# One PSUM bank for four products of a Winograd-style layer, and a unit's last additions spread over three quads

## The chip, the core and the metric

The kernel runs on one core of one Trainium2 chip. The core has a matrix engine (TensorE, "PE" in the profile, with its weight loads as "PEld"), VectorE ("DVE"), ScalarE ("ACT"), GpSimd ("POOL") and SyncE ("SP", here a queue for transfers). Each engine works through its own instructions in order, and engines wait for each other by semaphores. The metric is the device time of one execution in microseconds; lower is better.

## What is computed

Two layers in a row. The first filters each of 8 sequences along its length in the frequency domain; the second is a two-layer perceptron with an ELU between.

```python
# x: (8, 3008, 256), filt_r, filt_i: (1505, 256), w_in: (256, 2048), w_out: (2048, 256)
X = np.fft.rfft(x, axis=1)
y = np.fft.irfft(X * (filt_r + 1j * filt_i)[None], n=3008, axis=1)
h = y.reshape(8 * 3008, 256) @ w_in
g = np.where(h > 0, h, np.exp(np.minimum(h, 0)) - 1)
out = g @ w_out
```

Everything is float32; the two weight matrices and the filter arrive in the types that the kernel converts or gathers from.

## The kernel before

**The perceptron.** Both products are done by a 2 x 2 block scheme with seven products in place of eight (Strassen-Winograd). The rows of one batch are cut into six *units* (`m` = 0 to 5) of 2 x 256 rows (the first of 2 x 224), and the hidden width of 2048 into four parts (`q`). One combination of batch, unit and part is an *item*; there are 192. For an item, `up_steps` (line 296) gives seven steps s1 to s7 for the products P1 to P7 of the first layer, and `down_steps` (line 371) seven steps for the products of the second; below they are D1 to D7. One step is two matmuls of 128 x 128 weights with 256 columns, which the chip runs as four matmul records.

The seven first-layer products have to be added up. Before, P1 goes to PSUM tile pha and ScalarE copies it to t1; P2 is accumulated onto P1 in pha, which gives b11; P6 goes to phb and VectorE adds t1, giving t2; P5 goes to phc and VectorE adds t2, giving t4; P3 is accumulated in phc, and VectorE adds t2, giving b12; P7 goes to phd and VectorE adds t4, giving b22; P4 is accumulated in phd, and VectorE adds t2, giving b21. `add` is line 315. An accumulating step may write its tile only after whatever read the earlier sum there is done. On each of b11, b12, b22 and b21 the ELU runs as two ScalarE operations (`elu_exp`, lines 321 and 322: a Relu of -x, then an exponential) and one VectorE operation (`elu_max`, line 326). Four more VectorE operations (lines 359 to 363) combine these into the operands of the second layer's products: after them D1 takes b11, D2 b21, D3 b22, D4 t4, D5 t1, D6 t2 and D7 b12.

The second layer accumulates over the four parts `q` in four PSUM tiles po0 to po3. At the last part (`q == 3`), ScalarE copies po0 and po1 to k0 and k1 (line 387), VectorE makes one add (line 390) and, in the tail, six more (line 401) that give the unit's result c. `o_unit` (line 417) transposes c on VectorE (line 421) and issues 16 output transfers on SP.

**The order.** It is written out by hand. A loop over *quads* (line 626) runs the up steps of item i mixed with the down steps of item i - 1, by two strings of U and D; between the strings comes what a plan holds for "place 0" of that quad, and after the tails of both what it holds for "place 1". Since the down steps lag by one, unit m's last down steps run in the quad that is the next unit's first, numbered 4m + 4 within the batch's 24 quads.

```python
for k in "UDUDUDUUD": ...   # s1 D1 s6 D3 s2 D5 s5 s7 D7
                            # place 0
for k in "UDUDD": ...       # s3 D6 s4 D2 D4
                            # up_tail, down_tail, place 1
```

The plan spreads the filter layer of the following batch over the quads of this one: `a_unit` (first transform, place 0 of quads 0, 2, 3, 4, 6, 7), `b_unit` (second transform and the filter's four VectorE products, place 1 of quads 9 to 16), `bi_unit` (first half of the inverse, place 1 of quads 11 to 18), and `n_unit` (its second half and the rows' combination for one unit: 16 short matmuls, two ScalarE copies called y, four VectorE operations; place 0 of quads 8, 12, 16 and 20, place 1 of quads 1 and 5). `o_unit` stands at place 0 of quad 4m + 5 (counted from the batch's own start). The y rows that `n_unit` needs are read by `y_read` one or two quads ahead on the SP queue. In the first quads the conversion of the last weights (`w_convert`) and three memsets stand at place 1 of quads 0, 1 and 4.

**PSUM.** Eight banks: po0 to po3 hold one each, and a pool of four, `psM`, gives one to each of the other tiles in turn; every tile takes the buffer that was taken longest ago, and waits for its readers.

Of the kernel before, what the change touches and what calls it, by code (L numbers as in the profile page):

```python
# [95 lines left out]
def kernel(  # L96
# [30 lines left out]
    yd = pool("yd", 2, space=DRAM)  # L127
    fdp = pool("fdp", 1, space=DRAM)
    psO = pool("psO", 1, space=PSUM)
    psM = pool("psM", 4, space=PSUM)  # L130

    gb, gr, gi = (glob.tile([P, 2, 64], FP32, name=n) for n in ("gb", "gr", "gi"))

# [7 lines left out]

    def raw(src, row, ap, col=0):
        return bass.AP(tensor=src.tensor, offset=src.offset + row * D + col, ap=ap)

# [14 lines left out]
    def a_unit(b, c):  # L159
        t = t1s[b, c] = t1p.tile([P, XC, D], FP32, tag="t1", name="t1")  # L160
        xt, w = xs.pop((b, c)), tas.pop((b, c))
        for r in (0, 2):
            ps = psM.tile([P, 2, D], FP32, tag="mx", name="psa")
            for u in range(2):
                nc.tensor.matmul(ps[:, u, :], w[:, r + u, :], xt[:, r + u, :], start=True, stop=True)  # L165
            nc.scalar.activation(out=t[:, r:r + 2, :], in_=ps, func=AXT.Copy)

# [43 lines left out]
    def b_unit(b, g, f=None):  # L211
        t = t2s.pop((b, g))
        f = fbufs[(b * NG + g) % FBUFS] if f is None else f
        re, im = (psM.tile([P, 2, D], FP32, tag="mx", name=n) for n in ("psr", "psi"))
# [9 lines left out]
        nc.vector.tensor_tensor(out=q, in0=im, in1=f[:, 0], op=ALU.mult)  # L224
        nc.gpsimd.tensor_tensor(out=sr, in0=sr, in1=p, op=ALU.subtract)  # L225
        nc.gpsimd.tensor_tensor(out=si, in0=si, in1=q, op=ALU.add)
        ss[b, g] = (sr, si)

    def bi_unit(b, g):
        s = ss.pop((b, g))  # L230
        t = t3s[b, g] = t3p.tile([P, 4, D], FP32, tag="t3", name="t3")
        pa, pb = (psM.tile([P, 2, D], FP32, tag="mx", name=n) for n in ("pva", "pvb"))
# [4 lines left out]
        nc.scalar.activation(out=t[:, 2:4, :], in_=pb, func=AXT.Copy)  # L237

    def y_write(b, g):
        if g == 0:  # L240
# [16 lines left out]
    def n_unit(b, m):  # L257
        t, w, h = t4s.pop((b, m)), tns.pop((b, m)), half(m)
        rows = []
        for dh in range(2):  # L260
            y = yp.tile([P, 512], FP32, tag="y%d" % dh, name="y%d" % dh)
            ps = psM.tile([P, 512], FP32, tag="mx", name="psn")
# [3 lines left out]
            nc.scalar.activation(out=y[:, 0:2 * h], in_=ps[:, 0:2 * h], func=AXT.Copy)  # L266
            rows += [y[:, 0:h], y[:, h:2 * h]]
        s = yp.tile([P, 3, 256], FP32, tag="ys", name="ys")
        ys[b, m] = combine(*rows, *(s[:, i, 0:h] for i in range(3)))
# [23 lines left out]
    UPS = (1, 6, 2, 5, 7, 3, 4)  # L293
    DOWNS = (1, 3, 5, 7, 6, 2, 4)

    def up_steps(b, m, q):
# [7 lines left out]
        banks = {}  # L304

        def mm(n, key, start):
            if start:
                banks[key] = psM.tile([P, 2, 256], FP32, tag="mx", name="ph" + key)
            for a in range(2):
                nc.tensor.matmul(banks[key][:, a, 0:h], w_in[q][:, COMBO[n], a, :], y[n],  # L310
                                 start=start and a == 0, stop=True, skip_group_check=True)
            return banks[key][:, :, 0:h]

        def add(o, i0, i1):
            nc.vector.tensor_tensor(out=g[o], in0=i0, in1=i1, op=ALU.add)  # L315

        es = {}

# [8 lines left out]


        def s1():
            nc.scalar.activation(out=g["t1"], in_=mm(1, "a", True), func=AXT.Copy)  # L330

        def s6():
            add("t2", mm(6, "b", True), g["t1"])

        def s2():
            p = mm(2, "a", False)
            elu_exp("b11", p)
            elu_max("b11", p)

        def s5():  # L340
            add("t4", mm(5, "c", True), g["t2"])

        def s7():
            add("b22", mm(7, "d", True), g["t4"])
            elu_exp("b22", g["b22"])

        def s3():
            add("b12", mm(3, "c", False), g["t2"])
            elu_max("b22", g["b22"])

        def s4():
            elu_exp("b12", g["b12"])
            add("b21", mm(4, "d", False), g["t2"])

        def tail():
            elu_exp("b21", g["b21"])
            elu_max("b12", g["b12"])
            t1, b12, b22 = g["t1"], g["b12"], g["b22"]
            nc.vector.tensor_tensor(out=t1, in0=b12, in1=g["b11"], op=ALU.subtract)  # L359
            nc.vector.tensor_tensor(out=b12, in0=b22, in1=b12, op=ALU.subtract)  # L360
            elu_max("b21", g["b21"])
            nc.vector.tensor_tensor(out=g["t2"], in0=b22, in1=t1, op=ALU.subtract)
            nc.vector.tensor_tensor(out=g["t4"], in0=g["b21"], in1=g["t2"], op=ALU.subtract)
            g_of[b, m, q] = {1: g["b11"], 2: g["b21"], 3: b22, 4: g["t4"], 5: t1, 6: g["t2"], 7: b12}

        return (s1, s6, s2, s5, s7, s3, s4), tail


    PLACE = {1: (0, 0), 5: (0, 1), 3: (1, 0), 7: (1, 1), 2: (2, 0), 6: (2, 1), 4: (3, 0)}
# [1 line left out]
    def down_steps(b, m, q):  # L371
# [7 lines left out]
        def step(n):  # L379
            i, u = PLACE[n]  # L380
            for a in range(2):

                nc.tensor.matmul(po[i][:, u, 0:h], w_out[q][:, COMBO[n], a, :], g[n][:, a, :],  # L383
                                 start=q == 0 and a == 0 and n in (1, 3, 6, 4), stop=True, skip_group_check=True)
            if q == 3 and n in (5, 7):
                t = k[i] = kp.tile([P, 2, 256], FP32, tag="k%d" % i, name="k%d" % i)
                nc.scalar.activation(out=t[:, :, 0:h], in_=po[i][:, :, 0:h], func=AXT.Copy)
                if n == 7:
                    p3 = t[:, 0, 0:h]
                    nc.vector.tensor_tensor(out=p3, in0=p3, in1=k[0][:, 1, 0:h], op=ALU.add)  # L390

        def tail():
            if q != 3:
# [6 lines left out]
            def add(o, i0, i1):  # L400
                nc.vector.tensor_tensor(out=o, in0=i0, in1=i1, op=ALU.add)  # L401

            add(c12, po[2][:, 1, 0:h], p1)
            add(c11, po[2][:, 0, 0:h], p1)
            add(p7, p7, c12)
            add(c12, c12, p35)
            add(c21, po[3][:, 0, 0:h], p7)
            add(c22, p7, p5)
            cs_[b, m] = c

        return [(lambda n=n: step(n)) for n in DOWNS], tail

# [1 line left out]

    def o_unit(b, m):
        c = cs_.pop((b, m))
# [97 lines left out]
    with tc.manual_schedule():  # L516
# [81 lines left out]
        for b in range(B):  # L598
# [20 lines left out]
            for m, (s, place) in enumerate(((20, 0), (25, 1), (29, 1), (32, 0), (36, 0), (40, 0))):  # L619
                if b > 0 or m > 0:  # L620
                    at(t + s - (1 if m == 0 else 2), 0, y_read, b, m)
                    at(t + s, place, n_unit, b, m)
                at(t + PER + 4 * m + 5, 0, o_unit, b, m)

        items = [(b, m, q) for b in range(B) for m in range(6) for q in range(4)]
        for i in range(-PER, len(items) + 2):
            ups, up_tail = up_steps(*items[i]) if 0 <= i < len(items) else ((), None)
            downs, down_tail = down_steps(*items[i - 1]) if 1 <= i <= len(items) else ((), None)
            ups, downs = list(ups), list(downs)
            for k in "UDUDUDUUD":  # L630
                s = ups if k == "U" else downs
                if s:
                    s.pop(0)()
            for fn, a in plan.get((i, 0), ()):
                fn(*a)
            for k in "UDUDD":
                s = ups if k == "U" else downs
                if s:
                    s.pop(0)()
# [38 lines left out]
```

## Time and profile before

| what | value |
|---|---|
| median of 3 runs | 2736.13 us (2735.93 to 2737.07) |
| the profiled execution | 2735.2 us |
| its span, first to last instruction | 2733.4 us |
| first P1 of the first quad starts | 132.86 us |
| last matmul ends | 2721.3 us |
| mean granted clock of TensorE | 0.978 |

In the profile's group rows stand line, engine, operation, tiles (output, then inputs), shape and count; behind the first bar the busy time in us and the mean of one in ns; behind the second the engine's idle time just before them and what ended most of it. Matmul rows overlap, as a matmul starts before its predecessor has drained: the pace of TensorE is the distance from start to start, not the duration. In the timeline, "x4" says that four records were merged into one row. Half of the matmul records are of the second layer (L383), most of the rest of the first (L310).

```profile
L383 PE MATMUL po<-g,wo 128*128 128x256 f32 (+1 forms) x5376 | 1325.1, 375 | 0.0
L310 PE MATMUL pha<-y,wi 128*128 128x256 f32 (+1 forms) x1536 | 396.2, 380 | 9.3 <-ACT g L330 9.2
L322 ACT ACTIVATE e<-e 128x512 f32<-128x512 f32 (+1 forms) x768 | 477.5, 622 | 24.3
L326 DVE SCALAR_TENSOR_TENSOR g<-e,g 128x512 f32<-128x512 f32 (+1 forms) x576 | 387.0, 672 | 12.9 <-ACT e L322 12.8
```

### The profile page before, as it was taken

Reading aid. Unit: us, or ns where it says so; the run is one execution under the profiler, and the core shown is the slowest. Engines: PE = TensorE matmul, PEld = TensorE weight load, DVE = VectorE, ACT = ScalarE, POOL = GpSimd, SP = SyncE. Lnnn points to the kernel's source line nnn. Section 1 sums busy time; section 2 is a strip of 40 time slices with the busy share of each in tenths; the row PEclk is TensorE's granted clock in tenths of the full one; section 3 lists DMA queues with packets and bytes.
Section 4 is the critical chain, followed back from the end, with each engine's and each line's share of the span. In section 5 each row is a group of like instructions: output and inputs, shape, how many; then the busy total and the mean of one; then the engine's idle time right before and its main releaser. Section 6 shows DMA issues by size and latency. Waiting matters only on the chain.

```text
span 2733.4 us, 36388 instructions
## 1 busy us (share of the span) xinstructions
PE 2626.5 (96%) x12992; PEld 2237.5 (82%) x12992; DVE 2066.9 (76%) x3531; ACT 1286.0 (47%) x2177; POOL 275.6 (10%) x325
## 2 busy tenths in 40 slices
PE   2689999999999999999999999999999999999998
PEld 1278778987899878998789877898789987898887
DVE  3877877778777777768876787777877777777876
ACT  2244454544545444454444445454454544444443
POOL 4311210002000120001200021000210012000000
PEclk7599999999999999999999999999999999999999
DMA  9645321434114331242323333143421323110100
GB/s 244 180 116 122 88 69 37 110 96 102 43 42 121 78 93 37 74 120 68 79 50 88 88 85 73 37 110 97 98 57 41 79 62 95 37 39 19 26 22 16
DMA packets 229428, 214.47 MB, mean 78 GB/s; under 512 B 131620, under 2 KB 192566, under 8 KB 229248
## 3 DMA queue, kind: packets, MB, share of 16 engines
q1 hardware_dynamic: 210592, 173.65, 25.8%
q0 software_dynamic: 17792, 36.93, 5.6%
q8 instruction: 103, 1.69, 0.3%
q10 hardware_dynamic: 864, 1.57, 0.2%
q14 instruction: 77, 0.63, 0.1%
HBM read 136.97 MB, written 78.12 MB: 79 GB/s over the span
## 4 chain that ended last, share of the span: by engine, by line
PE 77%; DVE 12%; ACT 5%; DMA 2%; issue 2%; POOL 0%; DVEq 0%; SPq 0%; ACTq 0%; POOLq 0%
PE po L383 34%; PE pha L310 11%; PE phc L310 10%; PE phd L310 10%; PE phb L310 5%; DVE g L315 3%; PE psa L165 3%; ACT e L322 2%; ACT e L321 2%; PE pva L209 2%; PE psn L264 2%; PE psr L209 2%; DVE c L401 2%; DVE g L326 1%; DVE g L359 1%
## 5 line engine op out<-in xcount | busy, mean ns | idle before, releaser
L383 PE MATMUL po<-g,wo 128*128 128x256 f32 (+1 forms) x5376 | 1325.1, 375 | 0.0
L383 PEld LDWEIGHTS po<-g,wo 128*128 128x128 f32 x5376 | 1022.0, 190 | 116.4
L321 ACT ACTIVATE e<-g 128x512 f32<-128x512 f32 (+1 forms) x576 | 357.6, 621 | 616.2 <-DVE g L315 616.2
L322 ACT ACTIVATE e<-e 128x512 f32<-128x512 f32 (+1 forms) x768 | 477.5, 622 | 24.3
L310 PE MATMUL pha<-y,wi 128*128 128x256 f32 (+1 forms) x1536 | 396.2, 380 | 9.3 <-ACT g L330 9.2
L326 DVE SCALAR_TENSOR_TENSOR g<-e,g 128x512 f32<-128x512 f32 (+1 forms) x576 | 387.0, 672 | 12.9 <-ACT e L322 12.8
L315 DVE TENSOR_TENSOR g<-phc,g 128x512 f32<-128x512 f32 (+1 forms) x384 | 257.7, 671 | 141.3 <-PE phc L310 141.3
L321 ACT ACTIVATE e<-pha 128x512 f32<-128x512 f32 (+1 forms) x192 | 112.9, 588 | 532.5 <-PE pha L310 532.5
L310 PEld LDWEIGHTS pha<-y,wi 128*128 128x128 f32 x1536 | 285.3, 190 | 93.3 <-ACT t L236 34.1
L326 DVE SCALAR_TENSOR_TENSOR g<-e,pha 128x512 f32<-128x512 f32 (+1 forms) x192 | 129.4, 674 | 253.8 <-ACT e L322 253.8
L315 DVE TENSOR_TENSOR g<-phd,g 128x512 f32<-128x512 f32 (+1 forms) x384 | 260.6, 679 | 70.1 <-PE phd L310 50.0
L225 POOL TENSOR_TENSOR sr<-sr,sp 128x512 f32<-128x512 f32 x64 | 81.0, 1265 | 1289.4 <-DVE sp L223 1289.4
L310 PE MATMUL phc<-y,wi 128*128 128x256 f32 (+1 forms) x768 | 196.3, 378 | 5.0 <-DVE g L315 5.0
L310 PE MATMUL phc<-ys,wi 128*128 128x256 f32 (+1 forms) x768 | 195.3, 377 | 2.6 <-DVE si L222 2.6
L310 PE MATMUL phd<-y,wi 128*128 128x256 f32 (+1 forms) x768 | 194.7, 376 | 1.3
L310 PE MATMUL phd<-ys,wi 128*128 128x256 f32 (+1 forms) x768 | 194.2, 375 | 0.0
L310 PE MATMUL phb<-ys,wi 128*128 128x256 f32 (+1 forms) x768 | 193.8, 375 | 0.4 <-DVE ys L288 0.4
L310 PEld LDWEIGHTS phc<-y,wi 128*128 128x128 f32 x768 | 140.6, 190 | 29.5 <-DVE g L315 13.3
L310 PEld LDWEIGHTS phc<-ys,wi 128*128 128x128 f32 x768 | 145.3, 191 | 23.7 <-issue 7.8
L310 PEld LDWEIGHTS phd<-y,wi 128*128 128x128 f32 x768 | 144.7, 190 | 22.4 <-PE phc L310 6.5
L330 ACT ACTIVATE g<-pha 128x512 f32<-128x512 f32 (+1 forms) x192 | 112.7, 587 | 103.9 <-PE pha L310 103.7
L310 PEld LDWEIGHTS phd<-ys,wi 128*128 128x128 f32 x768 | 146.4, 191 | 16.7
(105 smaller groups left out, 2706.3 us busy)
## 6 DMA issues: line engine op xcount, KB each, us to landing
z<-t SPq DMA_DIRECT2D x192, 128.0 KB, 4.1
t<-z SPq DMA_DIRECT2D x128, 192.0 KB, 3.7
yd<-t SPq DMA_DIRECT2D x128, 192.0 KB, 2.8
t<-yd SPq DMA_DIRECT2D x192, 128.0 KB, 3.9
xc<-in_x_dram SPq DMA_DIRECT2D x84, 256.0 KB, 4.7
f<-fd POOLq DMA_DIRECT2D x112, 192.0 KB, 3.8
out_dram<-o SPq DMA_DIRECT2D x640, 32.0 KB, 1.6
tn<-tn_t SPq DMA_DIRECT2D x48, 256.0 KB, 3.8
```

What stands on the lines that cost most here:

```text
L165: nc.tensor.matmul(ps[:, u, :], w[:, r + u, :], xt[:, r + u, :], start=True, stop=True)
L209: nc.tensor.matmul(ps[:, u:u + w, :], table[k, v, :], rhs[k, u:u + w, :], start=True, stop=True)
L225: nc.gpsimd.tensor_tensor(out=sr, in0=sr, in1=p, op=ALU.subtract)
L264: nc.tensor.matmul(ps[:, ts(q, P)], t[:, i - 4 * m, ds(dh * P, P)], w[:, i - 4 * m, :], start=True, stop=True)
L310: nc.tensor.matmul(banks[key][:, a, 0:h], w_in[q][:, COMBO[n], a, :], y[n], start=start and a == 0, stop=True, skip_group_check=True)
L315: nc.vector.tensor_tensor(out=g[o], in0=i0, in1=i1, op=ALU.add)
L321: nc.scalar.activation(out=e, in_=src, func=AXT.Relu, scale=-1.0)
L322: nc.scalar.activation(out=e, in_=e, func=AXT.Exp, scale=-1.0)
L326: nc.vector.scalar_tensor_tensor(out=g[n], in0=es[n], scalar=1.0, in1=src, op0=ALU.subtract, op1=ALU.max)
L330: nc.scalar.activation(out=g["t1"], in_=mm(1, "a", True), func=AXT.Copy)
L383: nc.tensor.matmul(po[i][:, u, 0:h], w_out[q][:, COMBO[n], a, :], g[n][:, a, :], start=q == 0 and a == 0 and n in (1, 3, 6, 4), stop=True, ...
L401: nc.vector.tensor_tensor(out=o, in0=i0, in1=i1, op=ALU.add)
```

## The change

**First layer.** P1, P6, P5 and P3 are accumulated one after the other in a single PSUM tile, phs. ScalarE copies the partial sum out after P1 (t1), after P6 (t2) and after P5 (t4); after P3 the tile holds b12, and the ELU reads it there. P2 has a tile of its own, to which VectorE adds t1 (b11). b22 and b21 are formed in phd as before. So VectorE's adds of t2, t4 and b12 go, an add for b11 comes, and ScalarE's copies of t2 and t4 come. The copies stand in ScalarE's queue ahead of the exponentials of their quad.

**Order.** The steps now run s1 s2 D1 s6 D3 D5 s5, place 0, D7 s7 s3 D6 s4 D2 D4.

**A unit's end.** Both copies k0 and k1 are made after D7 instead of after D5 and D7. Three adds stay in the tail (the former line 390's among them); the other four move to place 0 of the following quad (`c_unit`), and `o_unit` with transposes and output transfers moves to place 0 of the quad after that.

**Banks.** The pool of four becomes four tags, and a list of free banks says which one a tile takes; a bank goes back to the end of the list where its last reader is issued.

```diff
+    banks = [0, 1, 2, 3]
+    def bank(name, shape=(P, 2, D)):
+        i = banks.pop(0)
+        return i, psM.tile(list(shape), FP32, tag="m%d" % i, name=name)
...
         def s1():
-            nc.scalar.activation(out=g["t1"], in_=mm(1, "a", True), func=AXT.Copy)
-        def s6():
-            add("t2", mm(6, "b", True), g["t1"])
+            keep("t1", mm(1, "s", True))
         def s2():
-            p = mm(2, "a", False)
-            elu_exp("b11", p)
-            elu_max("b11", p)
+            add("b11", mm(2, "a", True), g["t1"])
+            done("a")
+        def s6():
+            keep("t2", mm(6, "s", False))
         def s5():
-            add("t4", mm(5, "c", True), g["t2"])
+            keep("t4", mm(5, "s", False))
+            elu_exp("b11", g["b11"])
         def s7():
             add("b22", mm(7, "d", True), g["t4"])
-            elu_exp("b22", g["b22"])
+            elu_max("b11", g["b11"])
         def s3():
-            add("b12", mm(3, "c", False), g["t2"])
-            elu_max("b22", g["b22"])
+            p = mm(3, "s", False)
+            elu_exp("b12", p)
+            elu_exp("b22", g["b22"])
+            elu_max("b12", p)
+            done("s")
         def s4():
-            elu_exp("b12", g["b12"])
             add("b21", mm(4, "d", False), g["t2"])
+            done("d")
+            elu_max("b22", g["b22"])
         def tail():
             elu_exp("b21", g["b21"])
-            elu_max("b12", g["b12"])
...
-            if q == 3 and n in (5, 7):
-                t = k[i] = kp.tile(...)
-                nc.scalar.activation(out=t[:, :, 0:h], in_=po[i][:, :, 0:h], func=AXT.Copy)
-                if n == 7:
-                    p3 = t[:, 0, 0:h]
-                    nc.vector.tensor_tensor(out=p3, in0=p3, in1=k[0][:, 1, 0:h], op=ALU.add)
+            if q == 3 and n == 7:
+                for i in range(2):
+                    t = k[i] = kp.tile(...)
+                    nc.scalar.activation(out=t[:, :, 0:h], in_=po[i][:, :, 0:h], func=AXT.Copy)
...
+            add(p35, p35, p5)
             add(c12, po[2][:, 1, 0:h], p1)
             add(c11, po[2][:, 0, 0:h], p1)
-            add(p7, p7, c12)
-            add(c12, c12, p35)
-            add(c21, po[3][:, 0, 0:h], p7)
-            add(c22, p7, p5)
+            rest = [(p7, p7, c12), (c12, c12, p35), (c21, po[3][:, 0, 0:h], p7), (c22, p7, p5)]
+            cs_[b, m] = c, lambda: [add(*r) for r in rest]
...
-                at(t + PER + 4 * m + 5, 0, o_unit, b, m)
+                at(t + PER + 4 * m + 5, 0, c_unit, b, m)
+                at(t + PER + 4 * m + 6, 0, o_unit, b, m)
...
-            for k in "UDUDUDUUD":
+            for k in "UUDUDDU":
...
-            for k in "UDUDD":
+            for k in "DUUDUDD":
```

More of the change, by code (lines that the diff above doesn't have):

```diff
@@ L129 @@
     psO = pool("psO", 1, space=PSUM)
-    psM = pool("psM", 4, space=PSUM)
+    psM = pool("psM", 1, space=PSUM)
     gb, gr, gi = (glob.tile([P, 2, 64], FP32, name=n) for n in ("gb", "gr", "gi"))
@@ L162, in a_unit @@
         for r in (0, 2):
-            ps = psM.tile([P, 2, D], FP32, tag="mx", name="psa")
+            k, ps = bank("psa")
             for u in range(2):
@@ L166, in a_unit @@
             nc.scalar.activation(out=t[:, r:r + 2, :], in_=ps, func=AXT.Copy)
+            banks.append(k)
     def z_write(b, c):
@@ L213, in b_unit @@
         f = fbufs[(b * NG + g) % FBUFS] if f is None else f
-        re, im = (psM.tile([P, 2, D], FP32, tag="mx", name=n) for n in ("psr", "psi"))
+        (i0, re), (i1, im) = (bank(n) for n in ("psr", "psi"))
         for o, a in ((0, 0), (64, 2)):
@@ L224, in b_unit @@
         nc.vector.tensor_tensor(out=q, in0=im, in1=f[:, 0], op=ALU.mult)
+        banks.extend((i0, i1))
         nc.gpsimd.tensor_tensor(out=sr, in0=sr, in1=p, op=ALU.subtract)
@@ L231, in bi_unit @@
         t = t3s[b, g] = t3p.tile([P, 4, D], FP32, tag="t3", name="t3")
-        pa, pb = (psM.tile([P, 2, D], FP32, tag="mx", name=n) for n in ("pva", "pvb"))
+        (i0, pa), (i1, pb) = (bank(n) for n in ("pva", "pvb"))
         for o, table, sv in ((0, gr, s[0]), (64, gi, s[1])):
@@ L237, in bi_unit @@
         nc.scalar.activation(out=t[:, 2:4, :], in_=pb, func=AXT.Copy)
+        banks.extend((i0, i1))
     def y_write(b, g):
@@ L261, in n_unit @@
             y = yp.tile([P, 512], FP32, tag="y%d" % dh, name="y%d" % dh)
-            ps = psM.tile([P, 512], FP32, tag="mx", name="psn")
+            k, ps = bank("psn", (P, 512))
             for q, i in enumerate(order(m)):
@@ L266, in n_unit @@
             nc.scalar.activation(out=y[:, 0:2 * h], in_=ps[:, 0:2 * h], func=AXT.Copy)
+            banks.append(k)
             rows += [y[:, 0:h], y[:, h:2 * h]]
@@ L292 @@
     G_TAGS = (("g1", ("b11", "b12")), ("g2", ("b21", "b22")), ("g3", ("t1", "t2")), ("g4", ("t4",)))
-    UPS = (1, 6, 2, 5, 7, 3, 4)
+    UPS = (1, 2, 6, 5, 7, 3, 4)
     DOWNS = (1, 3, 5, 7, 6, 2, 4)
@@ L303, in up_steps, with done, keep @@
             g.update({n: t[:, i, :, 0:h] for i, n in enumerate(names)})
-        banks = {}
+        held = {}
         def mm(n, key, start):
             if start:
-                banks[key] = psM.tile([P, 2, 256], FP32, tag="mx", name="ph" + key)
+                held[key] = bank("ph" + key)
+            ps = held[key][1]
             for a in range(2):
-                nc.tensor.matmul(banks[key][:, a, 0:h], w_in[q][:, COMBO[n], a, :], y[n],
+                nc.tensor.matmul(ps[:, a, 0:h], w_in[q][:, COMBO[n], a, :], y[n],
                                  start=start and a == 0, stop=True, skip_group_check=True)
-            return banks[key][:, :, 0:h]
+            return ps[:, :, 0:h]
+        def done(key):
+            banks.append(held.pop(key)[0])
         def add(o, i0, i1):
             nc.vector.tensor_tensor(out=g[o], in0=i0, in1=i1, op=ALU.add)
+        def keep(o, i0):
+            nc.scalar.activation(out=g[o], in_=i0, func=AXT.Copy)
         es = {}
@@ L329, in s1, with s2, s3, s4 @@
         def s1():
-            nc.scalar.activation(out=g["t1"], in_=mm(1, "a", True), func=AXT.Copy)
+            keep("t1", mm(1, "s", True))
+        def s2():
+            add("b11", mm(2, "a", True), g["t1"])
+            done("a")
         def s6():
-            add("t2", mm(6, "b", True), g["t1"])
-        def s2():
-            p = mm(2, "a", False)
-            elu_exp("b11", p)
-            elu_max("b11", p)
+            keep("t2", mm(6, "s", False))
         def s5():
-            add("t4", mm(5, "c", True), g["t2"])
+            keep("t4", mm(5, "s", False))
+            elu_exp("b11", g["b11"])
         def s7():
             add("b22", mm(7, "d", True), g["t4"])
+            elu_max("b11", g["b11"])
+        def s3():
+            p = mm(3, "s", False)
+            elu_exp("b12", p)
             elu_exp("b22", g["b22"])
-        def s3():
-            add("b12", mm(3, "c", False), g["t2"])
+            elu_max("b12", p)
+            done("s")
+        def s4():
+            add("b21", mm(4, "d", False), g["t2"])
+            done("d")
             elu_max("b22", g["b22"])
-        def s4():
-            elu_exp("b12", g["b12"])
-            add("b21", mm(4, "d", False), g["t2"])
         def tail():
             elu_exp("b21", g["b21"])
-            elu_max("b12", g["b12"])
             t1, b12, b22 = g["t1"], g["b12"], g["b22"]
@@ L364, in tail @@
             g_of[b, m, q] = {1: g["b11"], 2: g["b21"], 3: b22, 4: g["t4"], 5: t1, 6: g["t2"], 7: b12}
-        return (s1, s6, s2, s5, s7, s3, s4), tail
+        return (s1, s2, s6, s5, s7, s3, s4), tail
     PLACE = {1: (0, 0), 5: (0, 1), 3: (1, 0), 7: (1, 1), 2: (2, 0), 6: (2, 1), 4: (3, 0)}
@@ L384, in step @@
                                  start=q == 0 and a == 0 and n in (1, 3, 6, 4), stop=True, skip_group_check=True)
[L385 to L390 removed]
+            if q == 3 and n == 7:
+                for i in range(2):
+                    t = k[i] = kp.tile([P, 2, 256], FP32, tag="k%d" % i, name="k%d" % i)
+                    nc.scalar.activation(out=t[:, :, 0:h], in_=po[i][:, :, 0:h], func=AXT.Copy)
         def tail():
@@ L401, in add, with c_unit @@
                 nc.vector.tensor_tensor(out=o, in0=i0, in1=i1, op=ALU.add)
+            add(p35, p35, p5)
             add(c12, po[2][:, 1, 0:h], p1)
             add(c11, po[2][:, 0, 0:h], p1)
-            add(p7, p7, c12)
-            add(c12, c12, p35)
-            add(c21, po[3][:, 0, 0:h], p7)
-            add(c22, p7, p5)
-            cs_[b, m] = c
+            rest = [(p7, p7, c12), (c12, c12, p35), (c21, po[3][:, 0, 0:h], p7), (c22, p7, p5)]
+            cs_[b, m] = c, lambda: [add(*r) for r in rest]
         return [(lambda n=n: step(n)) for n in DOWNS], tail
+    def c_unit(b, m):
+        cs_[b, m][1]()
     def o_unit(b, m):
-        c = cs_.pop((b, m))
+        c, _ = cs_.pop((b, m))
         o = op.tile([P, 16, 2, 32], FP32, tag="o", name="o")
@@ L622 @@
                     at(t + s, place, n_unit, b, m)
-                at(t + PER + 4 * m + 5, 0, o_unit, b, m)
+                at(t + PER + 4 * m + 5, 0, c_unit, b, m)
+                at(t + PER + 4 * m + 6, 0, o_unit, b, m)
         items = [(b, m, q) for b in range(B) for m in range(6) for q in range(4)]
-        for i in range(-PER, len(items) + 2):
+        for i in range(-PER, len(items) + 3):
             ups, up_tail = up_steps(*items[i]) if 0 <= i < len(items) else ((), None)
```

## The prediction

> **What bounds the kernel now.** I read the busy shares, then the groups, then the timeline of one undisturbed and one disturbed quad, then the lengths of all quads.
>
> ```profile
> PE 2626.5 (96%) x12992; PEld 2237.5 (82%) x12992; DVE 2066.9 (76%) x3531; ACT 1286.0 (47%) x2177; POOL 275.6 (10%) x325
> ...
> L315 DVE TENSOR_TENSOR g<-phc,g 128x512 f32<-128x512 f32 (+1 forms) x384 | 257.7, 671 | 141.3 <-PE phc L310 141.3
> ...
> L330 ACT ACTIVATE g<-pha 128x512 f32<-128x512 f32 (+1 forms) x192 | 112.7, 587 | 103.9 <-PE pha L310 103.7
> ```
>
> TensorE is the bound at 96%; VectorE has a quarter to spare, ScalarE half. The two lower rows price what is exchanged: a VectorE add from PSUM costs 0.671 us, a ScalarE copy from PSUM 0.587 us. Now the timeline (start, duration, engine, line, tiles; in brackets the idle time before), first an undisturbed quad, then the start of its successor:
>
> ```profile
> 2502.48 1.03 PE L310 MATMUL pha<-y,wi 128*128 128x256 f32 x4
> ...
> 2503.34 1.03 PE L383 MATMUL po<-g,wo 128*128 128x256 f32 x4
> 2503.54 0.60 ACT L330 ACTIVATE g<-pha 128x512 f32<-128x512 f32 x1 [0.57 <-PE pha L310]
> ...
> 2504.94 0.69 DVE L363 TENSOR_TENSOR g<-g,g 128x512 f32<-128x512 f32 x1
> ...
> 2514.57 1.03 PE L310 MATMUL pha<-y,wi 128*128 128x256 f32 x4
> ```
>
> A step (four matmul records) follows the last by 0.864 us, and 14 steps make 12.09 us (2514.57 - 2502.48): no gap at all. A step's result is taken 1.06 us after its start. The quad at 2528.44 is the one after a unit's end:
>
> ```profile
> 2532.49 0.75 DVE L401 TENSOR_TENSOR c<-po,k 128x256 f32<-128x256 f32 x2
> ...
> 2534.61 0.69 DVE L315 TENSOR_TENSOR g<-phb,g 128x512 f32<-128x512 f32 x1
> 2535.21 0.68 DVE L326 SCALAR_TENSOR_TENSOR g<-e,pha 128x512 f32<-128x512 f32 x1
> ...
> 2535.81 0.68 DVE L315 TENSOR_TENSOR g<-phc,g 128x512 f32<-128x512 f32 x1
> 2536.55 1.13 PE L310 MATMUL phc<-y,wi 128*128 128x256 f32 x4 [0.17 <-DVE g L315]
> ...
> 2540.97 0.59 PE L310 MATMUL pha<-y,wi 128*128 128x256 f32 x2
> ```
>
> VectorE works off six small adds of the finished unit (2532.49 to 2534.6), so its adds for this quad come late, and P3 may not enter phc before t4's add has read P5 there. The quad lasts 12.53 us: 0.34 lost in the wait, 0.10 in a slower restart. Taking every quad's start from the timeline in this way, the loss after 220 us lies in 34 quads, each the first of a unit: in each of the first seven batches quads 9, 13, 17 and 21 lose 0.44, 0.77, 0.76 and 0.26 us (in 13 and 17 filter products stand in VectorE's queue too), in the last batch six quads lose 0.42 to 0.66. Together **18.5 us**. Before 220 us: quad 5 takes 18.19 us against 13.87 for quad 5 of every later batch, 4.3 lost (2.5 of waiting on the same t4 add, behind three memsets, then matmuls at half speed); quad 1 waits 8.9 us for ScalarE, held by weight conversions; quad 2 waits 0.54 and 1.34. After the last matmul 12.1 us of additions, transposes and output remain. All else is matmuls without gaps, 132.9 us of opening included.
>
> **What the exchange costs.** Per quad two VectorE adds (t2, t4) go and two ScalarE copies come. VectorE: 13 operations to 11, 2066.9 - 384 x 0.671 = 1809 us (66%). ScalarE: 9 to 11, 1286 + 384 x 0.587 = 1511 us (55%). Matmuls stay 12992. By itself this is worth nothing, as neither engine is the bound; only waits of TensorE count. The Trainium skill speaks against it ("ScalarE: Activation LUTs", Rules for kernel authors): simple arithmetic belongs on VectorE, up to three times faster in bf16. If a copy so took an estimated 3 x 0.67 = 2.0 us, it would end 1.4 us later than below, about 0.5 us after its bank is wanted, three times a quad: 190 x 1.5 = 285 us lost. The rows, float32 from PSUM, say 0.59 against 0.67: I take the rows.
>
> **The new waits: one bank for four products.** Order by step: P1, P2, D1, P6, D3, D5, P5, [place 0], D7, P7, P3, D6, P4, D2, D4. P6, P5 and P3 must each wait until ScalarE has copied the sum before them. With R the start of P1: copy t1 1.06 to 1.66, P6 due 2.59; P6 read 3.65 to 4.25, P5 due 5.18; P5 read 6.24 to 6.84, P3 due 7.78. Release takes 0.06 (2535.81 + 0.68 to 2536.55), so each has 0.87 us of slack: cost 0. The page "PSUM — Partial Sum Buffer" (Summary: rules for kernel authors) says to read another bank than the one matmuls run into. Without work between, its price would be a result's 1.06 - 0.86, copy 0.60 and release 0.06, that is 0.86 us, 3 x 190 x 0.86 = 490 us. Two other steps (1.73 us) lie in each place and cover it.
>
> The copies need ScalarE free. Its last six operations (exponentials of b12, b22, b21) start at P3's result, 8.84, and at 0.63 to 0.66 each end at 12.76, 0.66 into the next quad, 0.40 before t1 is wanted. With the 0.87 above, ScalarE may be 1.27 us late before TensorE waits. Behind a waiting copy stand the exponentials, whose results the next quad's down steps need; these have over 1.5 us more.
>
> **VectorE in a plain quad.** b22's add 7.97 to 8.65; the next write to its bank, P4, is due at 9.50. Exponentials of b12 end 10.10, its max 10.14 to 10.82, b21's add to 11.5, b22's max to 12.15, four combinations and b21's max to 15.5, that is R + 3.4 in the next quad. Due are t1 by D5 (4.32), b12 by D7 (6.05), t2 by D6 (8.64): covered.
>
> **Where the 18.5 us go.** First quad of a unit: combinations end R + 3.4, three adds to 4.6, b11's add 5.3, place 0's other four adds 6.9, b22's add 7.97: no wait. In quads 13 and 17 TensorE does 1.88 us of filter steps before R: combinations end R + 1.6, three adds 2.7, four filter products 5.2, b11's add 5.9 (ScalarE wants it at 6.84), four adds 7.4, b22's add 7.97. No wait. The transposes (1.3 us) fall into the following quad, where only b11's add stands before them. Their 16 output transfers are now issued a quad later on SP, in quads that also hold y reads: 16 x 0.46 = 7.4 us of issue, begun some 6 us into the quad, end before 13.5; the five y-read transfers behind them still land some 12 us before their use. Cost 0; should it fail, unit's start waits for the y rows. Gain 18.5.
>
> **What is late next.** A quad with the next unit's transform at place 0 (31 of them; a unit ends there too): exponentials of b11 to 8.1, y copies 8.6 and 9.12, four VectorE combinations to 10.36, b22's add to 10.98, P4 due 11.28. Slack 0.3 less 0.06: the thinnest place of all. I take 0; the other bound is 0.25 late plus 0.10 restart, 31 x 0.35 = 10.9 us.
>
> **The opening.** Quad 0 has no down steps between the products: P5 waits for t2's copy (0.8), P4 0.1; the 0.5 that P6 waits there for its input row goes: +0.4. In quad 1 conversions start 0.7 later, of which 0.3 is new, and TensorE stops after three steps instead of four (0.76): +1.1. Quad 2: again a step earlier and later by the conversions (+0.9), but the 1.34 wait for a bank goes: -0.4. Quad 5: memsets end R + 7.75, b11's add 8.4, four adds 9.85, b22's add 10.5 against P4 due 9.50: 1.1 lost instead of 4.3, -3.2. Sum **-2.1** (bounds -4.3 and +2).
>
> **The end.** Both k copies now follow D7, the second some 0.57 us later, but the last adds wait for D4, 2.6 us after D7. The same four adds and transposes follow: 0 (0.3 either way).
>
> **Sum.** The profiled execution took 2735.2 us; - 18.5 - 2.1 = 2714.6. The median shown is 0.9 above it: **2715.5**.
>
> **Rivals.** *The wait moves.* The thin place gives: 2714.6 + 10.9 + 0.9 = 2726. For it: slack 0.24 rests on a chain of eight operations. Against: every duration is of the trace, and quads repeat to 0.01 us. *The shared bank binds (slower).* In every quad P6, P5 or P3 waits for a copy because ScalarE is late. It decides from 1.27 us of lateness, through b21's add held behind b12's max on VectorE; 0.11 us a quad eats the gain (20.6 / 190), and 0.1 late plus 0.1 restart gives 190 x 0.2 = 38 us: 2753. For it: ScalarE has 0.40 us between quads where it had pauses of 2 us. Against: 45% of its time is free. *The change doesn't do what it says:* VectorE stays late because another queue entry (the transposes' wait for earlier output, y reads) holds it: gain under 5 us, 2733.
>
> **Chances.** Forecast 0.72, wait moves 0.14, shared bank 0.09, no effect 0.05. No change means within 0.2%, 5.5 us, about what a measurement can tell. Faster 0.72 + 0.14 = 0.86, same 0.05, slower 0.09. The forecast's own range is 2710 (all of quad 5's loss and half of the opening's waits gone) to 2720; down a little and up to the first rival: 2709 to 2727.
>
> **What would show it.** Right: first quads of units at 12.1 us without a wait before P3, VectorE 66%, ScalarE 55%, quad 5 near 15. Wrong: TensorE waiting on the copy lines before P6, P5 or P3 in plain quads, or on b22's add before P4 in quads with a transform; or late y rows.

## The result, and the profile after

The changed kernel takes 2714.22 us (median of 4 runs, 2713.88 to 2714.39) against 2736.6 us before (2735.93 to 2737.75): a ratio of 0.9918, with a 95% interval of 0.990 to 0.9935. The prediction was 2715.5.

The page of the changed kernel, busy times and the chain that ended last:

```profile
PE 2618.7 (97%) x12992; PEld 2244.2 (83%) x12992; DVE 1809.0 (67%) x3147; ACT 1474.5 (54%) x2561; POOL 277.8 (10%) x325
...
PE 95%; DMA 2%; DVE 1%; issue 1%; ACT 0%; POOL 0%; SPq 0%; DVEq 0%; ACTq 0%; POOLq 0%
...
L334 ACT ACTIVATE g<-phs 128x512 f32<-128x512 f32 (+1 forms) x576 | 338.7, 588 | 844.5 <-PE phs L323 843.8
...
L323 PE MATMUL phs<-ys,wi 128*128 128x256 f32 (+1 forms) x1536 | 388.6, 375 | 11.2 <-ACT g L334 11.2
```

The same 12992 matmul records (5376 of each of the two layers, the rest of the filter); 384 operations less on VectorE, 384 more on ScalarE. The chain is now 95% TensorE; before, 12% of it was VectorE and 5% ScalarE:

```profile
PE 77%; DVE 12%; ACT 5%; DMA 2%; issue 2%; POOL 0%; DVEq 0%; SPq 0%; ACTq 0%; POOLq 0%
```

The last row of the first list is the one on which the change could have failed: P6 and P5 behind the copies out of their bank. It shows 11.2 us of waiting in all, and all of it lies in the first three quads; after 222 us the trace has no wait of TensorE at all.

The prediction calls the quads that lost time (9, 13, 17 and 21 of a batch) each the first of a unit. By the kernel's numbering they are the second, 4m + 5: in the first, 4m + 4, the finished unit's last down steps run, and their adds reach VectorE only after its tail. Below they are called the quads after a unit's end. One of them in the timeline of the changed kernel (quad 9 of the last batch, the same that starts at 2528.44 in the prediction):

```profile
2509.34 1.03 PE L323 MATMUL phs<-y,wi 128*128 128x256 f32 x4
...
2513.44 0.68 DVE L331 TENSOR_TENSOR g<-pha,g 128x512 f32<-128x512 f32 x1
...
2515.16 0.41 DVE L421 TENSOR_TENSOR c<-k,k 128x256 f32<-128x256 f32 x1
...
2517.38 0.69 DVE L331 TENSOR_TENSOR g<-phd,g 128x512 f32<-128x512 f32 x1 [1.80 <-ACT e L341]
...
2518.83 1.03 PE L323 MATMUL phd<-ys,wi 128*128 128x256 f32 x4
...
2521.42 1.03 PE L323 MATMUL phs<-y,wi 128*128 128x256 f32 x4
```

The quad lasts 12.08 us, a plain quad's length (2521.42 - 2509.34); it lasted 12.53. VectorE is done with the finished unit's seven adds (line 421) at 2515.57 and then has nothing to do for 1.8 us, until b22's add can start: P7's result is there at 2517.30 by the usual 1.06 us, and the exponential that the row names ended at 2517.35. That add ends at 2518.07, 0.76 before P4 starts.

Where the time went, by the starts of the first P1, of quad 6 and the end of the last matmul, as the timelines of both kernels give them:

| stretch | before, us | after, us | difference |
|---|---|---|---|
| start to first P1 | 132.86 | 134.31 | +1.45 |
| quads 0 to 5 | 89.90 | 86.17 | -3.73 |
| quad 6 to the last matmul | 2498.51 | 2479.93 | -18.58 |
| last matmul to the end | 12.17 | 12.17 | 0.00 |

### The profile page after: what moved, and what is told of

It reads as the page before. It is cut to its first block, busy times and chain, and to the rows that moved or that the text cites. A ratio compares the mean times of both kernels' runs of the same rounds, so it can differ in the third digit from the quotient of the medians.

```text
span 2712.6 us, 35960 instructions
## 1 busy us (share of the span) xinstructions
PE 2618.7 (97%) x12992; PEld 2244.2 (83%) x12992; DVE 1809.0 (67%) x3147; ACT 1474.5 (54%) x2561; POOL 277.8 (10%) x325
## 4 chain that ended last, share of the span: by engine, by line
PE 95%; DMA 2%; DVE 1%; issue 1%; ACT 0%; POOL 0%; SPq 0%; DVEq 0%; ACTq 0%; POOLq 0%
PE po L405 42%; PE phs L323 24%; PE phd L323 12%; PE pha L323 6%; PE psn L275 3%; PE psa L173 3%; PE pva L218 2%; PE psr L218 2%; DMA wb<-in_moe_w_in_dram 1%; DMA tb<-ta_t 0%; DMA ff<-in_filt_i_dram 0%; PE pvb L218 0%; DMA ff<-in_filt_r_dram 0%; DMA xb<-in_x_dram 0%; DVE wm L488 0%
## 5 line engine op out<-in xcount | busy, mean ns | idle before, releaser
L334 ACT ACTIVATE g<-phs 128x512 f32<-128x512 f32 (+1 forms) x576 | 338.7, 588 | 844.5 <-PE phs L323 843.8
L323 PE MATMUL phs<-ys,wi 128*128 128x256 f32 (+1 forms) x1536 | 388.6, 375 | 11.2 <-ACT g L334 11.2
L323 PE MATMUL phs<-y,wi 128*128 128x256 f32 (+1 forms) x1536 | 394.8, 379 | 0.0
L323 PEld LDWEIGHTS phs<-y,wi 128*128 128x128 f32 x1536 | 284.8, 190 | 82.9 <-ACT t L246 34.1
L323 PEld LDWEIGHTS phs<-ys,wi 128*128 128x128 f32 x1536 | 291.9, 190 | 45.5 <-ACT g L334 12.3
L345 DVE SCALAR_TENSOR_TENSOR g<-e,phs 128x512 f32<-128x512 f32 (+1 forms) x192 | 129.8, 676 | 138.6 <-ACT e L341 138.6
L340 ACT ACTIVATE e<-phs 128x512 f32<-128x512 f32 (+1 forms) x192 | 112.9, 588 | 161.6 <-PE phs L323 161.6
L323 PE MATMUL pha<-y,wi 128*128 128x256 f32 (+1 forms) x768 | 193.8, 375 | 0.0
L323 PEld LDWEIGHTS pha<-y,wi 128*128 128x128 f32 x768 | 145.8, 190 | 16.7 <-ACT y L277 0.2
L385 DVE TENSOR_TENSOR g<-g,g 128x512 f32<-128x512 f32 (+1 forms) x192 | 130.7, 681 | 6.6
L382 DVE TENSOR_TENSOR g<-g,g 128x512 f32<-128x512 f32 (+1 forms) x192 | 130.7, 681 | 6.6
```

Of the source, the lines that this page charges most:

```text
L323: nc.tensor.matmul(ps[:, a, 0:h], w_in[q][:, COMBO[n], a, :], y[n], start=start and a == 0, stop=True, skip_group_check=True)
L334: nc.scalar.activation(out=g[o], in_=i0, func=AXT.Copy)
L340: nc.scalar.activation(out=e, in_=src, func=AXT.Relu, scale=-1.0)
L345: nc.vector.scalar_tensor_tensor(out=g[n], in0=es[n], scalar=1.0, in1=src, op0=ALU.subtract, op1=ALU.max)
```

## The experiments

Theory A: in the quad after a unit's end VectorE's queue was too long in front of the operation that frees a bank, and nothing else was. Theory B: the two parts of the change (the first layer's bank scheme; the spread of the unit's end) are both needed for it. Beside these, the rivals of the prediction are put to the test: that the shared bank, or b22's add, is close to binding.

**The first layer alone.** The adds of a unit's end go back to the tail, its transposes to quad 4m + 5; the new order, the list of banks and the place of the k copies stay with the first layer:

```diff
-            rest = [(p7, p7, c12), (c12, c12, p35), (c21, po[3][:, 0, 0:h], p7), (c22, p7, p5)]
-            cs_[b, m] = c, lambda: [add(*r) for r in rest]
+            for r in [(p7, p7, c12), (c12, c12, p35), (c21, po[3][:, 0, 0:h], p7), (c22, p7, p5)]:
+                add(*r)
+            cs_[b, m] = c, None
...
-                at(t + PER + 4 * m + 5, 0, c_unit, b, m)
-                at(t + PER + 4 * m + 6, 0, o_unit, b, m)
+                at(t + PER + 4 * m + 5, 0, o_unit, b, m)
```

> First layer in one bank and the new order, but the unit's end as before: all seven adds in the tail, transposes one quad later. Theory A (VectorE's queue in a unit's first quad was too long, and either part of the change alone makes it short enough): combinations end R + 3.4, seven adds 6.1, b11's add 6.7, transposes 8.0, b22's add 8.7 against P4 due 9.5, so no wait; in quads 13 and 17 b22's add ends 9.4, a wait of 0 to 0.1; quad 5 of the start loses 1.4 more behind memsets and transposes: 2716 us (2714 to 2718). Theory B (the gain needs both parts, each alone brings about half): about 2725 us, with waits of TensorE for b22's add in first quads.

Measured: 2716.35 us (2715.26 to 2717.24), ratio 0.993 (0.9915 to 0.9945). From quad 6 to the last matmul 2480.04 us, against 2479.93 with both parts: no quad after a unit's end waits. Quad 5 takes 15.68 against 14.62 us, behind memsets and transposes, 1.1 more where 1.4 was expected. This run leaves all seven adds in VectorE's queue, but takes two other adds a quad off VectorE and has ScalarE's copy, not a VectorE add, free the bank for P3. Which of these is enough, and what the new order adds, was not tested apart.

**The unit's end alone.** The old first layer, order and pool of banks, with both k copies after D7, three adds in the tail, four at place 0 of the next quad, the transposes a quad later:

```diff
-            if q == 3 and n in (5, 7):
+            if q == 3 and n == 7:
+              for i in range(2):
...
+            add(p35, p35, p5)
             add(c12, po[2][:, 1, 0:h], p1)
             add(c11, po[2][:, 0, 0:h], p1)
+            rest = [(p7, p7, c12), (c12, c12, p35), (c21, po[3][:, 0, 0:h], p7), (c22, p7, p5)]
+            cs_[b, m] = c, lambda: [add(*r) for r in rest]
...
+                at(t + PER + 4 * m + 5, 0, c_unit, b, m)
+                at(t + PER + 4 * m + 6, 0, o_unit, b, m)
```

> First layer and order as before, only the unit's end spread over three quads. Theory A: in first quads three adds end R + 5.3, then t2's add, b11's max and t4's add end 7.2 against P3 due 7.78: no wait; in quads 13 and 17 t4's add ends 7.75, a wait of 0 to 0.1; quad 5 of the start loses 1.6 instead of 4.3: 2736.6 - 18.5 - 2.7 = 2716 us (2714 to 2718). Theory B: about 2725 us, P3 still waiting for t4's add in first quads.

Measured: 2718.25 us (2716.01 to 2718.48), ratio 0.9938 (0.9921 to 0.9954). The waits are gone here too: quads 9, 13, 17 and 21 last 13.21, 14.16, 13.30 and 12.09 us, as in the changed kernel. As only the unit's end was moved, this run shows VectorE's queue as their cause. But from quad 6 to the last matmul it takes 2483.87 us, 3.9 more. The only waits of TensorE after 222 us in the trace of this kernel:

```profile
PE pha L310 <- ACT t L236: 3.0, 14, 0.2
```

Fourteen times, at the end of quads 12 and 16 (16.23 us against 15.95), the next P1 waits for ScalarE's copy of a filter step. With both k copies behind D7, the y copies of the same quad come later on ScalarE (the first 10.18 us after the quad's start, 9.71 before), then the row combinations and b12's add on VectorE, and then b12's and b21's exponentials on ScalarE, which the filter copies stand behind:

```profile
309.62 1.06 ACT L388 ACTIVATE k<-po 128x512 f32<-128x512 f32 x2
...
310.57 1.08 ACT L266 ACTIVATE y<-psn 128x512 f32<-128x512 f32 x2
...
313.58 0.63 ACT L321 ACTIVATE e<-g 128x512 f32<-128x512 f32 x1 [1.93 <-DVE g L315]
```

The filter copy starts 15.59 us after the quad's start, 15.26 in the kernels before and after. In the changed kernel b12 needs no add, and the y copies stand ahead of the k copies, as place 0 comes before D7; which of the two keeps the copy in time was not tested. Theory B falls: either part removes the waits after a unit's end, and together they do not gain twice, since the same 18.5 us can be gained once. The 3.9 us of quads 12 and 16 were not lost before the change either; they are a cost of the spread in the old first layer, which the new one with its order does not have.

**The shared bank held longer.** t1 is copied out n times instead of once:

```diff
-            keep("t1", mm(1, "s", True))
+            p = mm(1, "s", True)
+            for _ in range(2):   # 3 in the next
+                keep("t1", p)
```

> The changed kernel with t1 copied out twice, so that the shared bank is held 0.53 us longer in each of 192 quads. My slack of 0.87 us: P6 is still in time, 2714 us (+0 to 0.5). The rival that the shared bank is near to binding (slack under 0.5): every quad waits, over 2725 us.

One profiled run, 2717.68 us. From quad 6 on 2479.93 us, to the hundredth what it is without the second copy. The two copies last 1.23 us together, so the bank was held 0.63 us longer, and the slack covered it. (Of the 3.3 us above the changed kernel's profiled run the first three quads, where conversions hold ScalarE anyway, lose 2.6; the other 0.7 lie ahead of the first P1.)

> t1 copied out three times: the bank is free at 1.06 + 0.53 + 0.53 + 0.60 + 0.06 = 2.78 after the quad's start, P6 due 2.59: 0.19 of wait and 0.10 of restart in 160 quads, 0.27 and 0.10 in the 32 narrower ones, 58 us: 2772 us. If ScalarE had more reach than I think (P6 not bound by the bank): 2714 us.

One profiled run, 2812.55 us: the bank binds, in every quad, but by 0.49 us instead of 0.29. The timeline of a plain quad that starts at 2767.22:

```profile
2768.28 1.86 ACT L334 ACTIVATE g<-phs 128x512 f32<-128x512 f32 x3 [0.41 <-PE phs L323]
...
2770.19 1.13 PE L323 MATMUL phs<-ys,wi 128*128 128x256 f32 x4 [0.22 <-ACT g L334]
```

Three copies last 1.86 us, so they follow each other by 0.63, not by the 0.53 that I had assumed. With 0.63, the bank is free 2.97 after the quad's start, where P6 does start (2770.19 - 2767.22); due 2.59, 0.38 of wait and 0.10 of restart. The slack of the prediction, 0.87, is confirmed from both sides: 0.63 us more fit into it, and of 1.26 us more 0.88 did. The miss is the spacing of these copies.

**P6 directly behind P1.** Nothing is left between two uses of the bank:

```diff
-        return (s1, s2, s6, s5, s7, s3, s4), tail
+        return (s1, s6, s2, s5, s7, s3, s4), tail
```

> The changed kernel with P6 directly behind P1 (and P2 after D1): nothing lies between two uses of the shared bank. My price: copy ends 1.66, release 0.06, P6 due 0.86, so 0.86 of wait and 0.10 of restart in 160 quads, 0.80 and 0.10 in 32 narrower ones: 182 us, 2896 us. If the reader of a bank did not hold back the next product: 2714 us.

One profiled run, 2896.22 us. Quads of 256 columns wait 0.85 and restart 0.10 slower, those of 224 0.80 and 0.10. The timeline of a quad:

```profile
2849.98 1.03 PE L323 MATMUL phs<-y,wi 128*128 128x256 f32 x4
...
2851.05 0.60 ACT L334 ACTIVATE g<-phs 128x512 f32<-128x512 f32 x1 [0.41 <-PE phs L323]
...
2851.70 1.13 PE L323 MATMUL phs<-ys,wi 128*128 128x256 f32 x4 [0.69 <-ACT g L334]
```

So the order of the steps is what makes one bank free of cost: one pair put together loses eight times what the change gained.

**More work ahead of b22's add.** In the quads with a transform at place 0, the last row combination is done three times:

```diff
-        ys[b, m] = combine(*rows, *(s[:, i, 0:h] for i in range(3)))
+        ys[b, m] = c = combine(*rows, *(s[:, i, 0:h] for i in range(3)))
+        if (b, m) != (0, 0) and m in (0, 3, 4, 5):
+            for _ in range(2):
+                nc.vector.tensor_tensor(out=c[4], in0=c[2], in1=c[6], op=ALU.subtract)
```

> The changed kernel with the last of a unit's row combinations done three times in the 31 quads that have the transform at place 0, which puts 0.72 to 0.80 us of VectorE in front of b22's add. The changed kernel's timeline leaves 0.35 there (add ends R + 10.88, release 0.06, P4 at R + 11.29): 0.4 of wait and 0.1 of restart, 31 x 0.5 = 15.5 us: 2730 us. With the slack of 0.24 that I had predicted: 31 x 0.62 = 19 us, 2733 us. If P4 does not hang on this add: 2714 us.

One profiled run, 2730.68 us; from quad 6 on 2499.67, 19.7 more than without. All 31 quads now wait at P4, by 0.58 and 0.10 (seven of them, where the combined rows have 224 columns, by 0.32 and 0.10). The two operations put b22's add 0.9 us later; 0.9 less 0.58 is the slack, a little over 0.3. This is the thinnest place of the changed kernel, and it holds.

**The conversions apart.** What is left of lost time lies in quads 0 to 5. A first try puts the last three weight conversions one to a quad, behind b22's add, and the memsets one to a quad:

```diff
-            at(max(k - 14, 0), 1, w_convert, k)
+            at(k - 13, 2, w_convert, k)      # place 2: after D7 s7
...
-            at(4, 1, nc.vector.memset, f, 0.0)
+            at(3 + j, 1, nc.vector.memset, f, 0.0)
```

> The changed kernel with the last three weight conversions one to a quad (0, 1, 2) between P7 and P3, behind b22's add on VectorE, instead of two at the end of quad 0 and one at the end of quad 1; the three memsets one to a quad (3, 4, 5). ScalarE's copy of t1 in quad 1 then no longer waits for the conversions: of 11.5 us (with the slow restart) in quad 1, 1.5 in quad 2 and 0.75 in quad 5 about 3 remain: 2704 us (2702 to 2709). If the conversions only wait elsewhere (down steps waiting for operands that VectorE forms late): 2711 us or more.

Measured: 2715.2 us (2714.33 to 2715.91), ratio 0.993 (0.9913 to 0.9946). Missed: quads 0 to 5 take 86.68 us, no less than without this edit (86.17). The waits moved: quad 1 takes 20.29 us instead of 23.88 and quad 2 13.31 instead of 13.81, but quad 3 now takes 17.68 instead of 12.32, with the same chain behind the third conversion. In quad 1 of this kernel, which starts at 142.11:

```profile
146.67 0.42 DVE L517 TENSOR_TENSOR wi<-wi 128x256 f32<-128x256 f32 x1
...
148.18 0.58 ACT L340 ACTIVATE e<-g 128x448 f32<-128x448 f32 x1 [3.34 <-DVE g L331]
...
149.85 1.86 PE L323 MATMUL phs<-ys,wi 128*128 128x224 f32 x4 [5.31 <-ACT g L334]
```

The conversion of quad 0 (ending 147.1) holds b21's add on VectorE (to 147.53). ScalarE stands idle for 3.34 us until b21's Relu, the first of its two operations there, can follow the add; behind the two stands t1's copy (149.27), and P6 waits for the copy. The expectation had named waits of the down steps as what could go wrong; it was an up step.

**The conversions in the gaps.** Between P6 and D3, so behind b11's add on VectorE and between two copies on ScalarE; the third is cut in half:

```diff
-        for k in (13, 14, 15):
-            at(max(k - 14, 0), 1, w_convert, k)
+        at(0, 2, w_convert, 13)
+        at(1, 2, w_convert, 14)
+        at(2, 2, w_convert, 15, (0,))
+        at(3, 2, w_convert, 15, (1,))
...
-            at(4, 1, nc.vector.memset, f, 0.0)
+            at(3 + j, 1, nc.vector.memset, f, 0.0)
...
+                if n == 3:           # place 2: after s1 s2 D1 s6
+                    for fn, a in plan.get((i, 2), ()):
+                        fn(*a)
```

> The changed kernel with the last three weight conversions between P6 and D3 of quads 0, 1 and 2 (the third in two halves, quads 2 and 3), behind b11's add on VectorE and between the copies of t2 and t4 on ScalarE, where both have 3 to 4 us free; memsets one to a quad (3, 4, 5). From the timeline of the changed kernel: conversion 14 ends R + 7.3 in quad 1, b22's add 7.95 against P4 due 8.34; first half in quad 2 ends R + 5.7, second half in quad 3 R + 6.7: no wait; quad 0 loses up to 1 more. So 11.5 + 1.5 + 0.75 go, 1 comes: quads 0 to 5 last 75 us instead of 86.2, and 2703 us (2700 to 2707). If the waits only move again, as with the conversions behind b22's add: 2711 us or more.

Measured: 2702.49 us (2700.65 to 2703.67), ratio 0.9879 (0.9863 to 0.9895), faster than both kernels. Quads 0 to 5 take 74.40 us. In quad 1 b22's add still comes a little late (P4 waits 0.6 us), and quad 0 loses some 1 us at the same place; in quads 2 to 5 no wait is left.

> The changed kernel once more, on the same chip as the conversions in gaps: 2714.2 us; quads from the sixth on last 2479.9 us to the last matmul again, and what differs from the first profile lies ahead of the first P1 (131 to 136 us after the start in the profiles so far).

Measured: 2714.68 us (2712.65 to 2716.55), on the same chip as the last. First P1 at 134.75, quads 0 to 5 86.07, from quad 6 to the last matmul 2479.93 us, as expected.

## Why the prediction was right

- **The gain.** 18.5 us were to go from the quads after a unit's end; 18.58 went, and no wait of TensorE is left after 222 us. The reading that found them, the length of every quad, is also what showed that they were gone.
- **Which waits they were.** Here the prediction had only one of two. It put the loss on P3, which waits for t4's add. The trace of the kernel before has two kinds of wait after 220 us:

```profile
PE phc L310 <- DVE g L315: 2.7, 13, 0.4
PE phc L310 <- DVE si L222: 2.6, 14, 0.2
```

The first is P3's. The second is P5's, in quads 13 and 17 of the first seven batches. There P5's tile takes the bank that filter products on VectorE still read, and the products stand behind the finished unit's adds:

```profile
2333.85 0.68 DVE L222 TENSOR_TENSOR si<-psr,f 128x512 f32<-128x512 f32 x1
...
2334.67 1.10 PE L310 MATMUL phc<-ys,wi 128*128 128x256 f32 x4 [0.19 <-DVE si L222]
```

P7 is then 0.33 us late once more; by the turn of the pool its bank is the one that the other two products read. These 14 quads hold 10.7 of the 18.5 us. The sum was right all the same, because both waits hang on the same queue: with the unit's end alone spread, and the pool of banks as it was, P5 in quads 13 and 17 starts 5.28 us after P1 instead of 5.64.
- **VectorE and ScalarE.** 1809 us were forecast for VectorE and 1809.0 measured. For ScalarE 1511 were forecast, 1474.5 measured. The copies did cost 0.588 us each; but operations that do not depend on each other overlap by some 0.1 us, which a sum of durations counts twice: summed up, ScalarE's durations rose by 222 us (1326 to 1548), its busy time by 188.5. In the changed kernel's timeline the ELU's first operation, a Relu, starts 0.11 before the copy ahead of it ends:

```profile
2501.71 0.60 ACT L334 ACTIVATE g<-phs 128x512 f32<-128x512 f32 x1 [1.99 <-PE phs L323]
2502.20 0.62 ACT L340 ACTIVATE e<-g 128x512 f32<-128x512 f32 x1
```

- **The rule against ScalarE.** A fall to 2 us a copy was weighed and refused on the row; the copy takes 0.588 us, and the rule's 285 us did not come.
- **The rule against one bank.** The price without cover, 0.86 us each time, was measured at 0.85 with P6 behind P1; with two steps between it is nothing, and with the bank held 0.63 us longer (the second copy) still nothing. Each of the forecast's parts, result, copy and release, stands.
- **VectorE's times.** b22's add was forecast 7.97 after such a quad's start and came at 8.04; b11's add ended at 4.8 (forecast 5.3), the last of four adds at 6.2 (6.9). I had added dependent spacings where operations overlap, in the safe direction.
- **What is late next.** The slack ahead of P4 in quads with a transform was put at 0.24 us and is a little over 0.3. The rival that lived on it was priced at 10.9 us and did not happen.
- **The opening.** -2.1 us was forecast for quads 0 to 5, -3.7 measured: quad 5 lost 0.75 instead of 1.1, quad 1 grew by 0.24 instead of 1.1. Against that stand 1.45 us ahead of the first P1, which the prediction did not have. That the profiled run, 2714.39, came within 0.3 us of the predicted 2714.6 is luck: these two nearly cancel, and the stretch ahead of the first P1 varies by 4 us between profiles (below).
- **The end** was forecast as unchanged, within 0.3: 12.17 us in both.

What the prediction did not say, as it summed over the whole change: either part alone removes the waits after a unit's end. It was right about the change, and would have been wrong as an account of what each part is worth.

## What to carry to other kernels

When an engine is busy for 96% and its gaps recur, measure the length of every round of the loop and look at the rounds that differ; the sum of their excess is the most that a reordering can bring there, and here it was 18.6 of the 20.8 us between the two profiled runs. Then look at what each late instruction waits for in every kind of such round: here two kinds of wait had one cause. Accumulating several products in one bank cost nothing here, as other matmuls lie between a product and the next one's use of the bank for longer than result, copy and release take together (1.73 us against 0.86) and the copying engine was free in time; moving one step of the order can make it cost 182 us. Before work is moved into another engine's gap, follow what stands behind it in every queue it passes through, to the next instruction of the bound engine: the conversions (with the memsets) moved to one place gained nothing, and to another 12 us.

## What the hardware showed beyond what was expected

- Copies of 128 x 512 float32 from PSUM on ScalarE start 0.48 us apart where they read different PSUM tiles and write different places (the two k copies above last 1.06 us together), and 0.63 apart where all read and write the same (1.86 us for three). Whether the common source or the common destination does it was not tested.
- After a wait of TensorE the matmuls start again either 0.10 us later than they should, or at half speed for some microseconds. Before the change, quad 5's wait of 2.53 us was followed by half speed: records 0.43 us apart where 0.22 is the pace, so that the four records of the next step took 1.71 us in place of 0.86.

```profile
214.86 1.45 PE L310 MATMUL phc<-y,wi 128*128 128x256 f32 x4 [2.37 <-DVE g L315]
216.10 1.91 PE L383 MATMUL po<-g,wo 128*128 128x256 f32 x4
```

With t1 copied three times, quad 2's wait of 2.54 us was followed by the full pace: the next eight records, of 224 columns, took 1.51 us.

All twelve waits from 2.9 to 11 us in the traces ended in half speed, waits up to 2.0 us never did. The granted clock in the traces tells the two waits of 2.5 us apart. In each trace it changes only at multiples of 3.41 us from one another, wherever the waits lie:

| kernel | stretch of 3.41 us | TensorE busy in it, us | granted clock in it | in the next stretch |
|---|---|---|---|---|
| before | 212.13 to 215.54 | 1.04 | 1.00 | 0.50 |
| t1 copied three times | 173.40 to 176.81 | 1.46 | 1.00 | 1.00 |

The first wait lies within one such stretch, the second is cut in two by the border at 173.40. From the first P1 to 240 us, all thirteen full-clock stretches of these traces in which TensorE was idle for 2.06 us or more were followed by half clock, and none with 1.95 or less. This is a count over the steps of the two layers only: ahead of the first P1, where the matmuls have other shapes, a full-clock stretch with 2.22 us of busy TensorE (changed kernel again) was followed by half clock too. The Trainium skill ("TensorE: Matmul & The Clock Gate", Part 1) tells of a window of about 3.4 us that runs freely, after an idle one of which the clock is halved. The free run agrees with these traces; that 2.06 us of idle time in a window are enough does not fit a whole idle one, and here the measurement decides.

- The stretch ahead of the first P1 varied from 131.2 to 135.4 us over the profiles of before, the changed kernel and its variants (eleven in all), whose code there differs at most in which PSUM buffer a tile takes. TensorE is busy for 57.9 of the first 132.9 us before the change (the prediction counted them among the matmuls without gaps); its largest waits in the changed kernel end with transfers, 31.6 us for z (what the first transform wrote), 13.1 for y, 11.3 for x. The variation, 4.2 us, is larger than what several of the edits above brought: quads and stretches of the trace tell apart what the totals can't. Why the stretch differs from run to run was not looked into.
